# Reading the first expert's rows ahead of a branch, sending the last records behind all rows, and laying the pools in another order

## The chip, the cores and the metric

The kernel runs on one core of one Trainium2 chip. The metric is device time in microseconds (us) of the whole program; the time of a kernel is the median of its runs. The engines are named as the profile names them: PE (matrix multiply; PEld is its weight load), DVE (vector), ACT (scalar), POOL (GpSimd) and SP (sync, which here issues nearly all transfers).

## The reference, cut to what matters

```python
attn_out = attn(q, k, v, s)              # 4 x 8 heads, 576 tokens, head 64, causal, with a decay bias
x = attn_out as (4, 576, 512)            # 2304 tokens of 512
# mixture of experts: every token goes to one of 8 experts
fresh_e = argmax(logits[b, s]);  e = fresh_e or the token's predecessor's expert, by local_gate
h = max(x[b, s] @ w1[e], 0);  out[b, s] = p[e] * (h @ w2[e])         # 512 -> 1024 -> 512
# mixer
h = x.T @ U @ V;  u = x + h.T
result = u + max(u @ w_ch1, 0) @ w_ch2                               # 512 -> 2048 -> 512
```

All of it is float32. The kernel splits a float32 operand into a high part and a low part (`xh`, `xl`; `hh`, `hl`; the two halves of a `ring` tile) and multiplies three of the four pairs.

## The kernel before

The program has three stages on the time axis of the profile: attention with the router (0 to about 313 us), the experts (about 329 to 598 us) and the mixer (about 601 to 1020 us). No scheduler orders the instructions: within an engine they run as the code emits them, and in the attention stage the table `ORDER` gives that order job by job (`issue(ORDER)`).

**The router** sorts the tokens by expert. Experts are ranked by their count of tokens, and the rows of the fullest one, which is done first, go to a buffer in device memory, `x0_d` (the trace calls it `x_d`). For every tile of 128 tokens POOL sends two scattered transfers (L1220): the rows themselves (`send_x`) and a record per token with its number, factor and mixer entries (`send_sd`, into `sd_d`). The last two groups of tokens (of three and of two tiles) are sent from about 310 us on. Behind `issue(ORDER)` SP reads four raw tiles of the first expert's second weight (`raw_out`, L216).

**Between router and experts** a count of tokens per expert, `cnt`, is made on DVE (L1697). Every engine then reads words of it into registers (`values_load`, L1706 and L1714; TENSOR_LOAD in the trace) and reaches a branch, `tc.If(over >= 0)` at L1720. What it guards treats tokens beyond an expert's capacity; with these inputs no expert has any, and every engine jumps over the guarded code. Behind the guarded code each engine passes a few semaphore instructions of L1720 that close it. An accumulator of the guarded code, `a_ext`, is zero then; it is the first operand of `pu`, the mixer's partial sum, by a matmul at L1849.

**The experts' start** lies behind the branch. In the order of the code: four `conv` calls split the four raw tiles into `ring10` to `ring13` (ACT casts the high part, L230; DVE subtracts for the low part, L233); SP reads the first expert's rows, `xrow0` to `xrow2`, from `x0_d` (L1998); SP reads two more raw tiles (L216) and the records of the expert (`load_sd`, L1872); POOL splits those two tiles. Then, for each of the three row tiles, PE turns it (`trans_x`, four transposes into `xps`, L1896) and `split_x` makes `xh` on ACT (L1901) and `xl` on DVE (L1902). `ffn` then multiplies: for each of the 8 slices of the hidden dimension 12 matmuls into `ps_h` (L1618; two buffers), a Relu split into `hh` and `hl` (L1581, L1582), and matmuls into `acc` (L1630). The first `ps_h` matmul takes `xh`, the second takes `xl`, of all three row tiles.

**Where tiles lie.** Tiles live in pools that are laid one behind another in the on-chip memory. A pool that is closed gives its place to one opened later, and an instruction that writes a tile then waits for what still uses the old one. `xh`, `xl` and `xrow` stand in the pool `mp`, which is opened behind the closed pools `gp` (of the branch) and those of attention; `ring10` to `ring13` stand in `wfix`.

Of the kernel before, what the change touches and what calls it, by code (L numbers as in the profile page):

```python
# [12 lines left out]
F32 = mybir.dt.float32  # L13
# [114 lines left out]
def kernel(  # L128
# [179 lines left out]
    with ExitStack() as ax:  # L308
        ap = ax.enter_context(tc.tile_pool(name="at1", bufs=1))
        a2 = ax.enter_context(tc.tile_pool(name="at2", bufs=2))  # L310
        a3 = ax.enter_context(tc.tile_pool(name="at3", bufs=3))
        xpool = ax.enter_context(tc.tile_pool(name="xpool", bufs=6))
        rp = ax.enter_context(tc.tile_pool(name="rp", bufs=3))
# [8 lines left out]
        def job(eng, cost, fn, after=(), takes=(), frees=()):  # L322

            jobs.append((eng, cost, fn, [a for a in after if a is not None], takes, frees))
            return len(jobs) - 1

        def issue(order):

            assert sorted(order) == list(range(len(jobs)))
            freer = {}  # L330
            for i, j in enumerate(jobs):
                for f in j[5]:
                    freer.setdefault(f, i)
            out, taken = set(), {k: [] for k in PLACES}
            for i in order:
                _, _, fn, after, takes, _ = jobs[i]
                assert all(a in out for a in after)
                for k in takes:
                    old = len(taken[k]) - PLACES[k]
                    assert old < 0 or freer[taken[k][old]] in out  # L340
                    taken[k].append(i)
                fn()
                out.add(i)
# [1038 lines left out]
        prev, ready_, ends = {}, {}, []  # L1382
        for gi, (b, ts) in enumerate(groups):
# [29 lines left out]
            for eng, cost, i, f, fn in sends:  # L1413
                if f is send_x:
                    need, frees = [done["where"], init_, normed[ts[i]][1]], (normed[ts[i]][0],)
                else:
                    need, frees = [done["where"], done["factor"], done["sides"]], ()
                ends.append(job(eng, cost, fn, need, (), frees))
            ready_[gi] = [x for x in done.values() if not isinstance(x, list)] + ends[-len(sends):]
            prev = done  # L1420
        issue(ORDER)
# [6 lines left out]

    c1f = [wfix.tile([P, 512], I32, name=f"c1f{i}") for i in range(NF2)]
    c1u = [wfix.tile([P, 2, 512], F16, name=f"c1u{i}") for i in range(NF2)]  # L1430
# [237 lines left out]

    ux = ExitStack()
    psu = ux.enter_context(tc.tile_pool(name="psu", bufs=1, space=PSUM))  # L1670
    pu = psu.tile([P, DM], F32, name="pu")
    with ExitStack() as gx:
        gp = gx.enter_context(tc.tile_pool(name="gp", bufs=2))
        gs = gx.enter_context(tc.tile_pool(name="gs", bufs=2, space=PSUM))
        a_ext = gp.tile([P, DM], F32, name="a_ext", bufs=1)
# [28 lines left out]
        )  # L1704
        who = [0] + [
# [143 lines left out]
        nc.tensor.matmul(pu, lhsT=ident, rhs=a_ext, start=True, stop=False)  # L1849

    NH = NF + 2
    fj = ctx.enter_context(tc.tile_pool(name="fj", bufs=1, reuse_waits="tile"))
    al = wfix.tile([P, DM], F32R, name="al")
    with ExitStack() as mx:
        mp = mx.enter_context(tc.tile_pool(name="mp", bufs=1, reuse_waits="tile"))
# [4 lines left out]
        xh = mp.tile([P, KD, CAP], F32R, name="xh")  # L1860
        xl = mp.tile([P, KD, CAP], F32R, name="xl")
        xrow = [mp.tile([P, DM], F32, name=f"xrow{i}") for i in range(NC_T)]
# [132 lines left out]
        for f in range(NEARLY, NEARLY + 4):  # L1995
            conv(w2u[f], raw0.pop(f), False, nc.scalar, nc.vector)
        for i, xe in enumerate(xrow):
            nc.sync.dma_start(xe, x0_d[i * P : (i + 1) * P])  # L1998
# [6 lines left out]
        for i, m in tiles_of(0):  # L2005
            split_x(trans_x(xrow[i], ps1 if i == 2 else psx), i, m)
        nc.gpsimd.tensor_copy(idx, side[:, :, TID])
# [333 lines left out]
```

## Time and profile before

| | us |
|---|---|
| runs | 1025.58, 1022.31, 1022.51 |
| median | 1022.51 |
| profiled execution | 1021.61 |
| its span (first to last instruction) | 1019.9 |
| PE busy in it | 954.7 (94%) |
| DVE, ACT, POOL busy | 569.1, 454.2, 360.6 |

The profiled execution lies 0.90 us under the median, and 1.71 us of it lie outside its span. The profile gives each instruction a start and a duration, names for an engine's idle time the instruction that ended it, and gives for a stretch of time the clock that PE was granted, as a share of full speed. All starts are us from the start of the span.

### The profile page before, as it was taken

The numbers are of one execution on the slowest core, as the hardware profiler recorded it, in microseconds if no ns is written. First come the engines' busy times: TensorE is split into PE (matmuls) and PEld (weight loads), VectorE is DVE, ScalarE is ACT, GpSimd is POOL, SyncE is SP. The second block draws the span as 40 slices with busy tenths as digits, with TensorE's granted clock in tenths as the row PEclk, the third lists the DMA queues.
The fourth block names the chain that finished last, engine by engine and source line by source line (L and its number), as shares of the span: only waits on it lengthen the run. The fifth ranks groups of instructions, "written<-read, shape, count | busy, mean of one in ns | idle before, by whom it ended". The sixth has DMA issues, their size and how long they took to land.

```text
span 1019.9 us, 17854 instructions
## 1 busy us (share of the span) xinstructions
PE 954.7 (94%) x6566; PEld 761.4 (75%) x6566; DVE 569.1 (56%) x1124; ACT 454.2 (45%) x1031; POOL 360.6 (35%) x460
## 2 busy tenths in 40 slices
PE   5887999999994999999999969999999999999998
PEld 4786978888882989888888857887666666666676
DVE  6666786676784677677675966883112312311121
ACT  4766876667761456556555753332112112211111
POOL 6623636246475465665667622220000000000000
PEclk9878998779985899999999989999999999999999
DMA  7988999686523765666665421421000200100010
GB/s 171 195 182 177 217 213 224 141 187 149 128 64 121 217 202 188 212 196 204 187 180 169 147 100 62 146 63 51 33 1 1 83 1 1 61 2 0 1 42 21
DMA packets 127424, 120.79 MB, mean 118 GB/s; under 512 B 58407, under 2 KB 99687, under 8 KB 125536
## 3 DMA queue, kind: packets, MB, share of 16 engines
q1 hardware_dynamic: 119264, 105.64, 39.4%
q0 software_dynamic: 6864, 13.63, 4.8%
q8 instruction: 54, 0.88, 0.4%
q10 hardware_dynamic: 1200, 0.30, 0.1%
q14 instruction: 42, 0.34, 0.1%
HBM read 76.84 MB, written 22.30 MB: 97 GB/s over the span
## 4 chain that ended last, share of the span: by engine, by line
PE 64%; DMA 1%; ACT 1%; POOL 1%; DVE 1%; issue 1%; SPq 0%; DVEq 0%; ACTq 0%; POOLq 0%
PE acc L1630 31%; PE ps_h L1618 29%; PE pu L1987 2%; PE ups L2210 1%; PE xps L1896 1%; DMA raw_out<-in_moe_w_dram 1%; PE ph L2161 0%; ACT y L2058 0%; POOL ring L233 0%; DMA ut<-yt_d 0%; DMA yt_d<-y,idx 0%; POOL ug L1924 0%; DVE ul L2213 0%; SPq L1998 0%; DVE ut L2281 0%
## 5 line engine op out<-in xcount | busy, mean ns | idle before, releaser
L1630 PE MATMUL acc<-ring,hh 128*128 128x512 f32 x928 | 301.5, 406 | 0.0
L1582 DVE SCALAR_TENSOR_TENSOR hl<-ps_h,hh 128x512 fp32r<-128x512 f32 (+6 forms) x144 | 82.3, 572 | 253.2 <-ACT hh L1581 253.0
L1581 ACT ACTIVATE hh<-ps_h 128x512 fp32r<-128x512 f32 (+6 forms) x144 | 72.7, 505 | 338.3 <-PE ps_h L1618 338.1
L1630 PEld LDWEIGHTS acc<-ring,hh 128*128 128x128 f32 x928 | 167.1, 185 | 37.8
L1618 PE MATMUL ps_h<-uh,c1u 128*128 128x256 f16 (+1 forms) x768 | 192.8, 330 | 1.4 <-ACT uh L2212 1.4
L1630 PE MATMUL acc<-ring,hl 128*128 128x512 f32 (+4 forms) x464 | 183.2, 395 | 0.0
L1618 PEld LDWEIGHTS <-c1u 128*128 128x128 f16 x1152 | 108.3, 99 | 86.1 <-issue 21.9
L1618 PE MATMUL ps_h<-ul,c1u 128*128 128x256 f16 (+1 forms) x384 | 126.2, 329 | 0.9 <-DVE ul L2213 0.9
L1618 PE MATMUL ps_h<-xh,ring 128*128 128x384 f32 (+5 forms) x512 | 125.5, 318 | 0.7 <-ACT xh L1901 0.7
L233 POOL TENSOR_TENSOR ring<-raw_out,ring 128x512 fp32r<-128x512 f32 x60 | 81.1, 1352 | 76.3 <-ACT ring L230 74.9
L1630 PEld LDWEIGHTS acc<-ring,hl 128*128 128x128 f32 (+4 forms) x464 | 85.7, 185 | 22.3 <-DVE hl L1582 0.4
L788 DVE SCALAR_TENSOR_TENSOR lo<-pp,hi 128x384 f16<-128x384 f32 (+2 forms) x160 | 85.7, 550 | 21.7 <-ACT hi L783 20.1
L2202 POOL TENSOR_SCALAR us<-ut,up 128x512 f32<-128x512 f32 x9 | 6.7, 739 | 252.9 <-DVE up L2186 252.9
L1618 PEld LDWEIGHTS ps_h<-xh,ring 128*128 128x128 f32 x512 | 90.3, 192 | 3.7 <-ACT xh L1901 1.1
L783 ACT ACTIVATE hi<-pp 128x384 f16<-128x384 f32 (+2 forms) x160 | 77.2, 496 | 31.1 <-PE pp L775 28.4
L775 PE MATMUL pp<-ident,Pb 128*128 128x128 f32 x480 | 87.4, 307 | 1.9 <-DVE lo L788 0.7
L705 PE MATMUL sp<-OP 128*128 128x288 f32 (+4 forms) x192 | 75.3, 396 | 8.9 <-DMA OP<-parts 4.4
L746 ACT ACTIVATE Pb<-sp,nm 128x192 f32<-128x192 f32 (+4 forms) x160 | 80.9, 537 | 5.0 <-DVE nm L729 3.9
L1618 PE MATMUL ps_h<-xl,ring 128*128 128x384 f32 (+5 forms) x256 | 80.9, 316 | 0.6 <-DVE xl L1902 0.6
L729 DVE TENSOR_REDUCE nm<-sp 128x1 f32<-128x576 f32 (+4 forms) x96 | 67.7, 705 | 18.9 <-PE sp L720 18.3
L233 DVE TENSOR_TENSOR ring<-raw_in,ring 128x512 fp32r<-128x512 f32 x56 | 57.7, 1031 | 34.6 <-ACT ring L230 34.4
L230 ACT CAST ring<-raw_out 128x512 fp32r<-128x512 f32 x60 | 36.9, 619 | 68.0 <-PE acc L1630 40.4
(249 smaller groups left out, 1639.6 us busy)
## 6 DMA issues: line engine op xcount, KB each, us to landing
raw_in<-in_moe_w_dram SPq DMA_DIRECT2D x64, 256.0 KB, 3.7
raw_out<-in_moe_w_dram SPq DMA_DIRECT2D x64, 256.0 KB, 4.0
raw<-in_moe_w_ch_dram SPq DMA_DIRECT2D x32, 512.0 KB, 4.2
OP<-parts SPq DMA_DIRECT2D x28, 576.0 KB, 6.7
OP<-parts SPq DMA_DIRECT2D x28, 288.0 KB, 6.5
kn<-in_k_dram SPq DMA_DIRECT2D x32, 128.0 KB, 6.1
x_d<-x SPq DMA_DIRECT2D x16, 256.0 KB, 3.1
out_dram<-ut SPq DMA_DIRECT2D x4, 1024.0 KB
```

What stands on the lines that cost most here:

```text
L230: hi_eng.copy(hi, src)
L233: lo_eng.tensor_tensor(out=lo, in0=src, in1=hi.bitcast(F32), op=ALU.subtract)
L705: nc.tensor.matmul(sp[:, c, :cw], lhsT=W1[j][:, h, t * P : (t + 1) * P], rhs=K1[j][:, h, c0 : c0 + cw], start=True, stop=False,)
L729: nc.vector.tensor_reduce(out=k["nm"] if two else k["nm"][:, 0:1], in_=k["sp"], op=ALU.min, axis=AX.X if two else AX.XY,)
L746: nc.scalar.activation(out_, in_, AF.Exp, scale=-1.0, bias=k["nm"][:, x : x + 1])
L775: nc.tensor.transpose(pp[:, i - i0], k["pb"][:, a, x * P : (x + 1) * P], ident)
L783: nc.scalar.activation(k["hi"][:, i0:i1], k["pp", i0][:, : i1 - i0], AF.Copy, scale=SCALE)
L788: nc.vector.scalar_tensor_tensor(out=k["lo"][:, i0:i1], in0=k["pp", i0][:, : i1 - i0], scalar=SCALE, in1=k["hi"][:, i0:i1], op0=ALU.mult, ...
L1581: nc.scalar.activation(hh[:, :n], ps[:, :n], AF.Relu)
L1582: nc.vector.scalar_tensor_tensor(out=hl[:, :n], in0=ps[:, :n], scalar=0.0, in1=hh[:, :n].bitcast(F32), op0=ALU.max, op1=ALU.subtract,)
L1618: nc.tensor.matmul(ps[f][:, x * cut : (x + 1) * cut], lhsT=wa[:, kk], rhs=xa[:, kk, :cut], start=(kk == 0 and i == 0), stop=(kk == KD - 1 ...
L1630: nc.tensor.matmul(acc[i][0:m], lhsT=ha[:, sl], rhs=u2[g][:, wa], start=(g == 0 and jj == 0), stop=(g == nf - 1 and jj == 2),)
```

## The change

1. In attention the pools `xpool` and `rp` are laid first instead of last, and in `wfix` the tiles `c1u` come ahead of `c1f`. No instruction moves by it; the addresses do.
2. The record sends of the last two groups are taken out of `ORDER` and issued behind all other jobs.
3. The three reads of `xrow` stand ahead of the reads of `cnt` and the branch (after.py L1681), and so do the four `conv` calls. The pool `mp` with `xh`, `xl` and `xrow` is opened ahead of `gp`.
4. `a_ext` moves from `gp` to the tile `al` of `wfix`, and its matmul into `pu` stands behind the twelve transposes of the rows.

```diff
@@ attention's pools
+        xpool = ax.enter_context(tc.tile_pool(name="xpool", bufs=6))
+        rp = ax.enter_context(tc.tile_pool(name="rp", bufs=3))
         ap = ax.enter_context(tc.tile_pool(name="at1", bufs=1))
         a2 = ax.enter_context(tc.tile_pool(name="at2", bufs=2))
         a3 = ax.enter_context(tc.tile_pool(name="at3", bufs=3))
-        xpool = ax.enter_context(tc.tile_pool(name="xpool", bufs=6))
-        rp = ax.enter_context(tc.tile_pool(name="rp", bufs=3))
@@ the router's jobs
-        prev, ready_, ends = {}, {}, []
+        prev, ready_, ends, last_ = {}, {}, [], []
...
                 ends.append(job(eng, cost, fn, need, (), frees))
+                if late and f is not send_x:
+                    last_.append(ends[-1])
...
-        issue(ORDER)
+        issue([i for i in ORDER if i not in last_] + last_)
         raw0 = {f: load_out(0, f) for f in range(NEARLY, NEARLY + 4)}
@@ wfix
+    c1u = [wfix.tile([P, 2, 512], F16, name=f"c1u{i}") for i in range(NF2)]
     c1f = [wfix.tile([P, 512], I32, name=f"c1f{i}") for i in range(NF2)]
-    c1u = [wfix.tile([P, 2, 512], F16, name=f"c1u{i}") for i in range(NF2)]
@@ ahead of the branch
+    al = wfix.tile([P, DM], F32R, name="al")
+    mx = ExitStack()
+    mp = mx.enter_context(tc.tile_pool(name="mp", bufs=1, reuse_waits="tile"))
+    xh = mp.tile([P, KD, CAP], F32R, name="xh")
+    xl = mp.tile([P, KD, CAP], F32R, name="xl")
+    xrow = [mp.tile([P, DM], F32, name=f"xrow{i}") for i in range(NC_T)]
+    for i, xe in enumerate(xrow):
+        nc.sync.dma_start(xe, x0_d[i * P : (i + 1) * P])
...
+    a_ext = al.bitcast(F32)
     with ExitStack() as gx:
...
-        a_ext = gp.tile([P, DM], F32, name="a_ext", bufs=1)
         nc.vector.memset(a_ext, 0.0)
...
+        for f in range(NEARLY, NEARLY + 4):
+            conv(w2u[f], raw0.pop(f), False, nc.scalar, nc.vector)
         who = [0] + [
@@ behind the branch
-        nc.tensor.matmul(pu, lhsT=ident, rhs=a_ext, start=True, stop=False)
...
-        for f in range(NEARLY, NEARLY + 4):
-            conv(w2u[f], raw0.pop(f), False, nc.scalar, nc.vector)
-        for i, xe in enumerate(xrow):
-            nc.sync.dma_start(xe, x0_d[i * P : (i + 1) * P])
...
         for i, m in tiles_of(0):
             split_x(trans_x(xrow[i], ps1 if i == 2 else psx), i, m)
+        nc.tensor.matmul(pu, lhsT=ident, rhs=a_ext, start=True, stop=False)
```

What stands on the engines in a row, at three places. Numbers behind a name tell tiles of one name apart; `x0_d_70` is the rows' buffer in device memory, `sd_d_71` the records'.

POOL, the last sends of the router, before:

```order
L1220 DMA x0_d_70<-x_5277,pos_5503 2304x512
L1220 DMA x0_d_70<-x_5386,pos_5503 2304x512
L1220 DMA sd_d_71<-sd_5496,pos_5503 18432x40 x2
L1220 DMA x0_d_70<-x_5283,pos_5475 2304x512
L1220 DMA sd_d_71<-sd_5450,pos_5475 18432x40 x3
```

and after:

```order
L1221 DMA x0_d_70<-x_5277,pos_5503 2304x512
L1221 DMA x0_d_70<-x_5386,pos_5503 2304x512
L1221 DMA x0_d_70<-x_5283,pos_5475 2304x512
L1221 DMA sd_d_71<-sd_5450,pos_5475 18432x40 x3
```

The last send of rows stands ahead of all five sends of records instead of behind two of them; the two of `sd_5496` now come last.

SP, from the raw tiles to the branch, before:

```order
L216 DMA raw_out_5544<-in_moe_w2_dram 128x512
L1706 TENSOR_LOAD cnt_5622 x7
L1714 TENSOR_LOAD cnt_5622
L1720 COMPARE_AND_BRANCH
```

SP behind the guarded code, before:

```order
L1720 UNCONDITIONAL_BRANCH
L1998 DMA xrow0_7022<-x0_d_70 128x512
L1998 DMA xrow1_7023<-x0_d_70 128x512
L1998 DMA xrow2_7024<-x0_d_70 128x512
L216 DMA raw_out_7036<-in_moe_w2_dram 128x512
```

and SP after, from the raw tiles to the branch:

```order
L216 DMA raw_out_5544<-in_moe_w2_dram 128x512
L1681 DMA xrow0_5611<-x0_d_70 128x512
L1681 DMA xrow1_5612<-x0_d_70 128x512
L1681 DMA xrow2_5613<-x0_d_70 128x512
L1722 TENSOR_LOAD cnt_5636 x7
L1730 TENSOR_LOAD cnt_5636
L1736 COMPARE_AND_BRANCH
```

The three reads of rows have changed sides with the eight reads of `cnt` and the branch.

PE, from the guarded code to the first expert, before:

```order
L1849 MATMUL pu_5605<-a_ext_5612,ident_73 128x512
L1896 MATMUL xps_7047<-ident_73,xrow0_7022 128x128 x4
L1896 MATMUL xps_7054<-ident_73,xrow1_7023 128x128 x4
L1896 MATMUL xps_7061<-ident_73,xrow2_7024 128x128 x4
L1618 MATMUL ps_h_7080<-xh_7020,ring0_80 128x384
L1618 MATMUL ps_h_7080<-xl_7021,ring0_80 128x384
```

and after:

```order
L1903 MATMUL xps_7045<-ident_73,xrow0_5611 128x128 x4
L1903 MATMUL xps_7052<-ident_73,xrow1_5612 128x128 x4
L1903 MATMUL xps_7059<-ident_73,xrow2_5613 128x128 x4
L2010 MATMUL pu_5620<-al_5605,ident_73 128x512
L1621 MATMUL ps_h_7079<-xh_5609,ring0_80 128x384
L1621 MATMUL ps_h_7079<-xl_5610,ring0_80 128x384
```

The matmul into `pu` has passed the twelve transposes and stands directly ahead of the first `ps_h` matmul.

## Rows read from the trace of the kernel before

**Rows 1.** Page, part 1: PE's busy time, share of the span, instructions.

```profile
PE 954.7 (94%) x6566; PEld 761.4 (75%) x6566; DVE 569.1 (56%) x1124; ACT 454.2 (45%) x1031; POOL 360.6 (35%) x460
```

**Rows 2.** Timeline of PE at the experts' start: start, us, work [idle before <-what ended it].

```profile
322.03 2.04 PE L1849 MATMUL pu<-a_ext,ident 128*128 128x512 f32 x2 [8.52 <-DMA x_d<-x,pos]
325.00 1.09 PE L1896 MATMUL xps<-ident,xrow 128*128 128x128 f32 x4 [0.92 <-DMA xrow<-x_d]
326.66 1.97 PE L1896 MATMUL xps<-ident,xrow 128*128 128x128 f32 x8 [0.57 <-DMA xrow<-x_d]
329.31 0.69 PE L1618 MATMUL ps_h<-xh,ring 128*128 128x384 f32 x1 [0.67 <-ACT xh L1901]
330.60 0.69 PE L1618 MATMUL ps_h<-xl,ring 128*128 128x384 f32 x1 [0.61 <-DVE xl L1902]
```

**Rows 3.** Waits of PE from 331 to 600 us: total, times, longest.

```profile
PE pu L1987 <- ACT yh L2071: 2.7, 3, 1.4
```

**Rows 4.** Chain of waits that ends at 330.60: start, us, what.

```profile
324.43 3.99 DMA raw_out<-in_moe_w_dram
...
328.66 0.67 DVE xl L1902
```

**Rows 5.** Timeline of SP around the branch: start, us, transfers issued.

```profile
322.10 1.76 SPq L1998 DMA_DIRECT2D xrow<-x_d  x3
323.91 0.91 SPq L216 DMA_DIRECT2D raw_out<-in_moe_w_dram  x2
```

**Rows 6.** Timeline of POOL, the last sends: start, us, send, idle before.

```profile
316.40 0.97 POOL L1220 DMA_INDIRECT sd_d<-sd,pos  x1 [0.30 <-issue]
...
318.96 0.97 POOL L1220 DMA_INDIRECT x_d<-x,pos  x1 [0.30 <-issue]
320.24 0.97 POOL L1220 DMA_INDIRECT sd_d<-sd,pos  x1 [0.31 <-issue]
...
322.82 1.50 POOL L1220 DMA_INDIRECT sd_d<-sd,pos  x1 [0.30 <-issue]
```

**Rows 7.** Tile x_d, 309 to 323 us: from a send to its landing.

```profile
DMA to landing us min/median/max: 2.3/2.3/2.9
```

**Rows 8.** SP's reads of cnt: count, ns min/median/max, first and last start.

```profile
L1706 SPq TENSOR_LOAD <-cnt x7: 263/272/473, 315.7 to 317.8; - x7
```

**Rows 9.** The branch (L1720) by engine: count, ns min/median/max, first and last start.

```profile
L1720 SPq EVENT_SEMAPHORE  x9: 17/17/17, 321.1 to 321.7; - x9
L1720 POOLq EVENT_SEMAPHORE  x5: 17/43/5047, 322.3 to 327.6; - x5
L1720 ACTq EVENT_SEMAPHORE  x2: 17/17/17, 319.6 to 319.7; - x2
L1720 DVEq EVENT_SEMAPHORE  x2: 21/21/21, 320.7 to 320.8; - x2
L1720 PEldq EVENT_SEMAPHORE  x2: 51/51/51, 321.2 to 321.3; - x2
...
L1720 DVEq COMPARE_BRANCH  x1: 72/72/72, 317.6 to 317.6; - x1
L1720 SPq COMPARE_BRANCH  x1: 50/50/50, 318.5 to 318.5; - x1
```

**Rows 10.** Timelines of DVE and ACT around the branch: start, us, work.

```profile
320.98 2.50 DVE L233 TENSOR_TENSOR ring<-raw_out,ring 128x512 fp32r<-128x512 f32 x4 [5.36 <-DMA x_d<-x,pos]
328.66 1.89 DVE L1902 TENSOR_TENSOR xl<-xps,xh 128x512 fp32r<-128x512 f32 x3 [5.18 <-DMA raw_out<-in_moe_w_dram]
...
319.91 2.18 ACT L230 CAST ring<-raw_out 128x512 fp32r<-128x512 f32 x4 [10.32 <-DMA sd_d<-sd,pos]
```

**Rows 11.** Stretches of PE: us, busy (instructions), granted clock, DMA share, GB/s.

```profile
610.90:616.50 5.60, 5.59 (x27) 0.50 0.00 1
...
330.60:336.60 6.00, 6.00 (x19) 0.50 0.97 290
336.70:339.70 3.00, 3.00 (x19) 1.00 0.84 245
```

More of the change, by code (lines that the diff above doesn't have):

```diff
@@ L1665, in ffn @@
         return acc
+    NH = NF + 2
+    fj = ctx.enter_context(tc.tile_pool(name="fj", bufs=1, reuse_waits="tile"))
+    al = wfix.tile([P, DM], F32R, name="al")
[6 more added lines that the diff above has]
+        nc.sync.dma_start(xe, x0_d[i * P : (i + 1) * P])
     ux = ExitStack()
@@ L1847 @@
                     )
-        nc.tensor.matmul(pu, lhsT=ident, rhs=a_ext, start=True, stop=False)
[L1851 to L1855, printed above, removed]
+    with mx:
         m3 = mx.enter_context(tc.tile_pool(name="m3", bufs=3, reuse_waits="tile"))
@@ L1859 @@
         psx = mx.enter_context(tc.tile_pool(name="psx", bufs=2, space=PSUM, reuse_waits="tile"))
-        xh = mp.tile([P, KD, CAP], F32R, name="xh")
-        xl = mp.tile([P, KD, CAP], F32R, name="xl")
-        xrow = [mp.tile([P, DM], F32, name=f"xrow{i}") for i in range(NC_T)]
         def tiles_of(j):
```

## The prediction

> **What bounds the kernel now.** I read the busy times first. PE works for 954.7 us, 94% of the span [rows 1], so a gain must be found where PE waits, or where its clock is low. Then the waits of PE from the experts' start on: behind 331 us the longest entry in its list is 2.7 us in three waits [rows 3], and so what starts there earlier also ends earlier: a gain at the start of the experts carries to the end at full size. Third, PE's timeline of that start [rows 2]. The reader is to see five pieces with a gap ahead of each: 8.52 us of waiting for the router's sends and the branch, `pu` at 322.03, a gap of 0.92 until the first row tile is there (325.00), 0.57 until the others are (326.66), 0.67 until `xh` is made, and 0.61 until `xl` is. From 330.60 on PE runs without gaps. Without that last gap the same row would have begun at 330.60 - 0.69 = 329.91; this is the moment that I compare with.
>
> What holds each piece? The chain of waits [rows 4] names for the last gap a transfer of `raw_out`, issued at 324.43 and landed 3.99 later; `xl` doesn't read it. The tile `xl` lies on a place that the branch's pool had, and waits for transfers of the time before. The rows themselves hang on `xrow`, issued from 322.10 on [rows 5]. Two things end there nearly at once: SP comes out of the branch (semaphore instructions until 321.7 [rows 9]), and the last send of rows, started at 318.96 [rows 6], lands 2.3 to 2.9 us later [rows 7], at 321.3 to 321.9. Neither alone would bring much; the change moves both.
>
> **The sends.** On POOL the last send of rows takes the place of a record send at 316.40 instead of 318.96 [rows 6]: 2.56 us earlier, with landing at 318.7 to 319.3. The number of sends is the same, so the last ends where it did, and POOL's part of the branch's end, which waits for the landings until 327.6 [rows 9], stays.
>
> **The reads of the rows.** SP now meets them ahead of its reads of `cnt`. It has nothing else to do then: those reads begin at 315.7 [rows 8], when `cnt` is there. So `xrow` goes out when the last send has landed. If the landing was what held it before (2.9), it goes 2.56 earlier, at 319.5; if the branch held it (2.3), it goes at 318.9, 3.2 earlier. I take 2.8 between the two, 319.3. Queued behind it on SP are seven reads of `cnt` of 0.27 us each and the branch. Before, this was 315.7 to 318.5, then the jump until 321.1 and semaphores until 321.7 [rows 8, 9]: 2.8 + 2.6 + 0.6 = 6.0. The three reads take 1.76 [rows 5], so SP comes out at 319.3 + 1.8 + 6.0 = 327.1, and the two `raw_out` behind it go out 3.2 later than 323.91. Who waits for that is POOL, which splits them into tiles needed six and seven slices later, each many microseconds long, and the first Relu, below.
>
> **The transposes.** From the issue to the first tile it took 325.00 - 322.10 = 2.9 us, to the others 326.66 - 322.10 = 4.6. Moved rigidly by 2.8, PE turns the first tile at 322.2 and the others from 323.9 to 325.8. If all landed 2.9 after their own issue, the end would be 325.2. PE is out of the branch at 321.3 and ACT at 319.7 [rows 9], before that. DVE needs a look: its four `conv` subtracts, 2.50 us [rows 10], now stand ahead of its branch, which it reached at 317.6 and left at 320.8; it will leave at about 323.3, which is ahead of the third tile's transposes and of `xl`. ACT's four casts [rows 10] fall into an idle stretch of 10.32 us and cost nothing.
>
> **The matmul into `pu`.** It moves 2.04 us [rows 2] from a stretch in which PE waited to one in which it could work, so by itself it costs. It covers the making of `xh` (0.67) and `xl` (0.61), whose false wait is gone since `mp` no longer lies on the branch's pool. The first `ps_h` matmul comes at 325.8 + 2.04 = 327.9, with the better landings at 327.3, and nothing waits behind it. Against 329.91 that is 2.0 to 2.6 earlier; I take 2.3. The sum in parts: 2.8 for the rows, 0.67 and 0.61 for the two gaps, less 2.04, makes 2.0, and 0.3 for a part of the better landings.
>
> **The clock.** PE was granted half speed until 336.60, 6.00 us behind the start of the row without gaps, and there 19 matmuls took 6.00; behind it 19 took 3.00 [rows 11]. The same was seen at the other low place: dense from 610.9, full from 616.5, 5.60 later. So each microsecond at the low level costs half of one. Before, 336.60 - 329.91 = 6.7 us of the experts' work were done low. Now the row without gaps is longer ahead of the first `ps_h`. If `pu` counts in it, it starts at 325.8 and the clock returns at about 331.8, 3.9 behind 327.9: 2.8 fewer low, worth 1.4. If only the experts' matmuls count, 6.0 are low and 0.35 is won; if the transposes from 323.9 count too, 2.0 are low and 2.35 is won. I take 1.4, the middle.
>
> **Addresses.** The reordered pools and `c1u` ahead of `c1f` add no instruction; they serve that `conv` and `xrow` can run early without a wait for a late tile of attention. Their price is nothing by itself; if they fail, that is the second rival below.
>
> **The sum.** 2.3 + 1.4 = 3.7 us. The profiled execution has 1021.61, so 1017.9; the median of the runs lies 0.90 above that execution, which makes 1018.8. The ends of the unknowns: 2.0 + 0.35 = 2.35 and 3.0 (reads at 318.9 with the better landings) + 2.35 = 5.35, that is 1020.2 and 1017.2.
>
> **The rivals.** First, *a new last wait eats a part*. The send at 316.40 now lies beside the four subtracts of DVE, which would run from about 315.7 to 318.2. Before, these subtracts (320.98 to 323.48) lay beside three record sends of 0.97, 1.00 and 1.50 [rows 6, 10]: at most 0.53 was lost, and the sends kept their spacing of 1.3. So I price this at 0 to 0.53. Were a send held until the subtracts are done, it would start at 318.2, 1.8 later, and leave 3.7 - 1.8 = 1.9: 1020.6. [...] To the same case belong a landing of a row tile slower than before by 1 to 2 us and a DVE that leaves its branch later than the third tile is turned. They leave 1 to 2.6, at 1019.9 to 1021.5. For it speaks that 4.6 us for the later tiles already show transfers in each other's way.
>
> Second, *the rows don't come earlier*: something else (a place in memory that a late tile still holds) keeps `xrow` until about 322. Then the transposes end at 328.63 as before, `pu` runs until 330.7, 0.8 behind 329.91, and the clock, counted from `pu` as above, gives back 1.4: a gain of 0.6, at 1021.9. Against it: the waits of the moved reads in the built program are those for the sends alone.
>
> Third, on the other side, *SP comes out of the branch too late*. The first Relu waits for SP's part of the branch's end; SP now waits for the rows' landing ahead of its jump. PE can fill two `ps_h` tiles, 24 matmuls of 0.316 [rows 11], from 327.9 to 335.5, before it needs the first Relu's result, which takes some 0.6. The loss begins when SP comes out later than 334.9, against my 327.1; it cancels the gain from 338.6 on, 11.5 later than I reckon, and each microsecond behind that makes the kernel one slower than before. It needs a jump or a landing several times longer than any in the rows (jumps of 2.6 to 3.1 for SP and DVE, landings up to 3.99), so it is unlikely.
>
> **How the numbers follow.** The forecast has 0.62, the new last wait 0.21, rows not earlier 0.10, SP too late 0.07. What a measurement of this kernel can tell from no change is about 0.3%, 3.07 us: faster means below 1019.4. The forecast lies 0.6 below that; of its 0.62 I put 0.54 below and 0.08 above, where the clock gives little. Within 0.3% falls that 0.08, with the first two rivals and 0.01 of the last: 0.40. Slower gets 0.06. The range takes in the ends of the sum and the first rival; it leaves out the last rival and most of the second, some 0.16, and reaches from 1017.0 to 1021.6.
>
> **What the profile of the changed kernel would show.** The last send of rows at 316.4, not 318; `xrow` issued at 319 to 319.5 (322 would be the second rival); transposes from about 322.2; `pu` directly behind them, and the first `ps_h` at 327.3 to 327.9 with no gap behind; the granted clock full from about 331 to 332 (333.9 would take away 1.0 of the gain); SP out of its branch near 327, and no wait of PE for a Relu before 336. Wrong would be a gap of PE behind the first `ps_h` matmul, or a time outside the range.

## The result, and the profile after

The changed kernel takes 1014.23 us (median of 6 runs, 1007.95 to 1017.78), the kernel before beside it 1024.42 (6 runs). The ratio of the two is 0.9903, with a 95% interval of 0.9881 to 0.9926: some 9.9 us faster. That is the forecast direction, but 2.7 times the 3.7 us forecast, and it lies below the range. The runs of the changed kernel also spread over 10 us, those of the kernel before over 3.

The profiled execution of the changed kernel took 1015.48 us, with a span of 1013.5: 6.4 less than the span before. PE's line of the page beside [rows 1]:

```profile
PE 936.4 (92%) x6566; PEld 743.1 (73%) x6566; DVE 567.8 (56%) x1124; ACT 453.6 (45%) x1031; POOL 361.6 (36%) x460
```

To see where the 6.4 us lie, cut both spans at two instructions of DVE: the one that ends `cnt`, behind all of attention and the router, and the one that reads `pu` for the mixer, behind all experts. DVE's timelines, before first (start, us, work):

```profile
315.46 0.16 DVE L1697 TENSOR_SCALAR cnt<-cnt 1x8 int32<-1x8 int32 x1
...
600.64 0.68 DVE L2103 TENSOR_TENSOR mix<-pu,mix 32x512 fp32r<-32x512 f32 x1 [0.51 <-ACT mix L2102]
```

and after:

```profile
309.87 0.16 DVE L1711 TENSOR_SCALAR cnt<-cnt 1x8 int32<-1x8 int32 x1
...
595.22 0.68 DVE L2107 TENSOR_TENSOR mix<-pu,mix 32x512 fp32r<-32x512 f32 x1 [0.51 <-ACT mix L2106]
```

| us | before | after | difference |
|---|---|---|---|
| start to `cnt` ready (attention, router) | 315.62 | 310.03 | -5.6 |
| `cnt` ready to `pu` read (the handover and the experts) | 285.02 | 285.19 | +0.2 |
| `pu` read to the end (mixer) | 419.26 | 418.29 | -1.0 |

So in this pair of profiles nearly all of the gain lies in attention, where no instruction moved but for the last sends, and none in the stretch from `cnt` to `pu`, at which the moved instructions aim ("the stretch" below; a number with a plus, such as +9.3, is us behind `cnt`). In the first 300 us PE was granted a mean of 0.93 of full speed instead of 0.88, and was busy 256.40 us instead of 266.09 (stretches: us, PE busy, clock, DMA share, GB/s; before, then after):

```profile
0.00:300.00 300.00, 266.09 (x2934) 0.88 0.79 172
```

```profile
0.00:300.00 300.00, 256.40 (x2979) 0.93 0.74 173
```

The handover itself did change. PE's timeline after, beside [rows 2]:

```profile
319.33 2.79 PE L1903 MATMUL xps<-ident,xrow 128*128 128x128 f32 x12 [11.38 <-DMA xrow<-x_d]
321.91 1.27 PE L2010 MATMUL pu<-al,ident 128*128 128x512 f32 x2
322.80 0.57 PE L1621 MATMUL ps_h<-xh,ring 128*128 128x384 f32 x1
323.52 0.44 PE L1621 MATMUL ps_h<-xl,ring 128*128 128x384 f32 x1 [0.16 <-DVE xl L1909]
...
333.85 0.44 PE L1621 MATMUL ps_h<-xh,ring 128*128 128x384 f32 x1 [1.77 <-DVE hl L1585]
```

Transposes, `pu` and `ps_h` now follow each other with one gap of 0.16 instead of three of 0.57 to 0.67. But the transposes begin 319.33 - 310.03 = 9.30 us behind `cnt`; before it was 325.00 - 315.62 = 9.38. And 11 us on there is a new gap of 1.77. The clock came back much earlier, at about 322.4, 12.4 behind `cnt` instead of 21.0 (stretches of PE after, beside [rows 11]):

```profile
300.00:322.30 22.30, 7.40 (x39) 0.50 0.31 98
322.50:336.00 13.50, 11.57 (x59) 1.00 0.64 183
```

### The profile page after: what moved, and what is told of

Read it like the earlier page. It is cut to its first block, busy times and chain, and to the rows that moved or that the text cites. A ratio compares the mean times of both kernels' runs of the same rounds, so it can differ in the third digit from the quotient of the medians.

```text
span 1013.5 us, 17840 instructions
## 1 busy us (share of the span) xinstructions
PE 936.4 (92%) x6566; PEld 743.1 (73%) x6566; DVE 567.8 (56%) x1124; ACT 453.6 (45%) x1031; POOL 361.6 (36%) x460
## 4 chain that ended last, share of the span: by engine, by line
PE 63%; DMA 2%; DVE 1%; ACT 1%; issue 1%; SPq 0%; POOL 0%; DVEq 0%; ACTq 0%; POOLq 0%
PE acc L1633 31%; PE ps_h L1621 28%; PE pu L1994 2%; PE ups L2214 1%; DMA raw_in<-in_moe_w_dram 1%; PE xps L1903 1%; DMA raw_out<-in_moe_w_dram 0%; PE ph L2165 0%; DVE c1u L1536 0%; DMA yt_d<-y,idx 0%; DMA ut<-yt_d 0%; ACT y L2062 0%; DVE ul L2217 0%; POOL ring L233 0%; DVE ut L2285 0%
## 5 line engine op out<-in xcount | busy, mean ns | idle before, releaser
L776 PE MATMUL pp<-ident,Pb 128*128 128x128 f32 x480 | 83.8, 297 | 4.7 <-DVE lo L789 2.6
L706 PE MATMUL sp<-OP 128*128 128x288 f32 (+4 forms) x192 | 71.8, 379 | 7.9 <-DMA OP<-parts 3.2
L713 PE MATMUL sp<-OP 68*128 68x288 f32 (+4 forms) x192 | 61.4, 324 | 2.2 <-DMA OP<-b_d 2.2
## 6 DMA issues: line engine op xcount, KB each, us to landing
OP<-parts SPq DMA_DIRECT2D x28, 288.0 KB
```

The source lines that it names most:

```text
L706: nc.tensor.matmul(sp[:, c, :cw], lhsT=W1[j][:, h, t * P : (t + 1) * P], rhs=K1[j][:, h, c0 : c0 + cw], start=True, stop=False,)
L713: nc.tensor.matmul(sp[:, c, :cw], lhsT=W2[j][0:SK, h, t * P : (t + 1) * P], rhs=K2[j][0:SK, h, c0 : c0 + cw], start=False, stop=not diag,)
L776: nc.tensor.transpose(pp[:, i - i0], k["pb"][:, a, x * P : (x + 1) * P], ident)
```

## The experiments

Three questions: what made attention shorter; why the rows came no earlier; and what the moved instructions are worth in the end. Ratios are to the kernel before in the same series of runs, since the kernel before itself took 1014 to 1022 us in the other series; the absolute times expected of the first four kernels were reckoned from the 1024 of the result, but the kernel before took 1016.33 beside them, so only the ratios are compared.

**What made attention shorter.** The reordered pools move attention's pool `at1` (its tiles `kn`, `qn`, `vn` and `OP` are filled by transfers) from byte 69024 of each partition to 96000: from 160 past a multiple of 256 to a multiple of 256. Two kernels move only that pool, one moves it back in the changed kernel, and one makes the first part of the change alone. The shift, ahead of `at1` (a second one behind it makes the two add up to 512 bytes for all that follows):

```diff
+        pada = ax.enter_context(tc.tile_pool(name="pada", bufs=1))
+        pada.tile([P, 24], F32, name="pada")
         ap = ax.enter_context(tc.tile_pool(name="at1", bufs=1))
```

The kernel before, shifted by 96:

> The kernel before, with 96 unused bytes per partition laid ahead of the pool at1 and 416 behind it; no instruction moves. at1 holds attention's tiles that transfers fill (kn, qn, vn, OP); it began at byte 69024, 160 past a multiple of 256, and begins at 69120, a multiple of 256, as in the changed kernel (96000). Theory A: the addresses make attention shorter (in the first 100 us the packets of the hardware queue took 53.6 ns each before, 75.2% of 16 engines for 22456 packets, and 47.3 ns after, 68.0% for 22980; cnt was ready 5.6 us earlier). It expects packets near 47 ns, cnt ready at 306 to 312 us instead of 315.5, and a time of 1014 to 1020. Rival B: attention's shorter time is chance of one profile or comes from the order of the code, and the gain is that of the moved reads: 53 ns, cnt at 315, 1022 to 1026.

The kernel before, shifted by 32 (`[P, 8]`):

> The kernel before, with 32 unused bytes ahead of at1 and 480 behind: at1 begins at 69056, a multiple of 64 but 192 past a multiple of 256. If a multiple of 64 is what the transfers want, it does as the shift by 96 does (packets near 47 ns in the first 100 us, 1014 to 1020). If it is a multiple of 256, packets stay at 52 to 55 ns and the time at 1021 to 1026. Rival B expects 1022 to 1026 too, but then for the shift by 96 as well.

The changed kernel, shifted by 160 (`[P, 40]`):

> The changed kernel, with 160 unused bytes ahead of at1 and 352 behind: at1 begins 160 past a multiple of 256 again, as in the kernel before; all instructions stand as changed. Theory A: attention is as long as before (cnt ready at 314 to 317 us, packets near 53 ns), and what is left is the gain of the moved reads, sends and pu, 0 to 4 us by what the trace of the changed kernel shows (7.0 earlier at the first ps_h matmul of which 5.6 are attention's, 3.3 of clock, and some 4 lost again to waits until 373 us): 1019 to 1024. Rival B: 1012 to 1017 as the changed kernel.

The pools alone, that is the kernel before with the first point of the change and nothing else:

> The kernel before with the first part of the change alone: xpool and rp laid first, c1u ahead of c1f. at1 begins at 96000, a multiple of 256. Theory A: as the shift by 96, 1014 to 1020, cnt ready at 306 to 312. Rival B (the gain comes from the reads ahead of the branch): 1022 to 1026, cnt at 315.

Measured: 0.9937 (0.9901 to 0.9972) for the shift by 96; 0.9996 (0.9969 to 1.0023) for the shift by 32; 0.992 (0.9888 to 0.9953) for the pools alone; 0.9994 (0.9965 to 1.0022) for the changed kernel shifted off. `cnt` was ready at 304.95, 312.24, 309.05 and 311.18 in their profiles; the last lies below the 314 to 317 that were expected of it. Over all profiles of this document it was 304.8 to 314.5 with `at1` at a multiple of 256 (13 profiles, mean 309.6) and 311.2 to 315.6 off it (four, mean 313.1), so a single pair of profiles, like that of the result, shows little. The transfers separate the kernels clearly. The row of the hardware queue over the first 100 us (packets, MB, share of 16 engines), for before, after, the shifts by 96 and by 32, and the changed kernel shifted by 160:

```profile
q1 hardware_dynamic: 22456, 15.20, 75.2%
```

```profile
q1 hardware_dynamic: 22980, 15.51, 68.0%
```

```profile
q1 hardware_dynamic: 22980, 15.51, 68.4%
```

```profile
q1 hardware_dynamic: 22243, 14.86, 75.8%
```

```profile
q1 hardware_dynamic: 22966, 15.50, 75.5%
```

Share times 16 engines times 100 us, by packets: 53.6, 47.3, 47.6, 54.5 and 52.6 ns a packet. All kernels with `at1` at a multiple of 256 lie at 47 to 49, all others at 52.6 to 54.5. The rival, that the moved reads made the whole gain, falls: without the addresses 0.6 us is left of it, give or take 3, and the addresses alone give most. A multiple of 64 wasn't enough (54.5 ns a packet, 0.9996). A start 128 past a multiple of 256 was not tried, so these runs can't tell a boundary of 256 bytes from one of 128.

The higher clock of the first pair, 0.93 against 0.88 over the first 300 us, can't be put down to the addresses: over all profiles it was 0.89 to 0.94 with `at1` at a multiple of 256 and 0.88 to 0.93 off it (0.89 in `e3_pools_only`, 0.93 in `q_moves` below). In which waits of attention the shorter packets save time wasn't followed.

**Do more addresses help?** The raw weights, too, begin 160 past a multiple of 256. `f1_all_aligned` is the changed kernel with all bulk tiles at multiples of 256:

```diff
+    padc = ctx.enter_context(tc.tile_pool(name="padc", bufs=1))
+    padc.tile([P, 24], F32, name="padc")
     wring = ctx.enter_context(tc.tile_pool(name="wring", bufs=1))
...
+        pada = ax.enter_context(tc.tile_pool(name="pada", bufs=1))
+        pada.tile([P, 40], F32, name="pada")
         ap = ax.enter_context(tc.tile_pool(name="at1", bufs=1))
...
     al = wfix.tile([P, DM], F32R, name="al")
+    wfix.tile([P, 24], F32, name="padw")
```

> The changed kernel with unused bytes laid in (96 ahead of wring, 160 ahead of at1, 96 at the end of wfix), so that all tiles that transfers fill or empty in bulk begin at multiples of 256: the raw weights (160 past one before and changed), the x rows (160 past one in the changed kernel), xrow and the raw tiles of the mixer's weights (64 past one). If the addresses matter for these too, attention is 0 to 2 shorter than in the changed kernel, the landings of raw tiles are shorter, the waits of PE among the experts (0.5 to 4 us in the changed kernel) shrink, and the time is 2 to 5 below the changed kernel's (0.980 to 0.988 of the kernel before). If only attention's small packets mind, it is as the changed kernel (0.988 to 0.993).

Measured 0.9908 (0.9877 to 0.9938), as the changed kernel. The raw weights' packets are of 512 and 2048 bytes, and they took as long as elsewhere: from 340 to 580 us a mean of 27.5 and 96.6 ns, against 27.6 and 95.2 in the changed kernel and 27.7 and 97.3 before. `f0_before_all_aligned` has the same addresses, with all instructions in the old order:

> The kernel before with the pools of the change and the unused bytes of f1_all_aligned, but no instruction moved: all addresses are good, sends, reads, conv and pu stand as before. If the addresses are the whole gain: 0.989 to 0.992 as f1. If the moved instructions give 1.5 to 3 us besides (the stretch from cnt to the end of the experts was 285.1 in the mean of four kernels with the old order, 283.6 in three with the new, and the mixer 0.9 shorter): 0.992 to 0.995, and the stretch is 284.8 to 285.5.

Measured 0.9921 (0.9892 to 0.9951); its stretch was 288.0, out of what was expected. I come back to that.

**Why the rows came no earlier.** The last send of rows did start 2.5 us earlier, 0.81 behind `cnt` instead of 3.34. After, POOL's row, and SP's rows at the reads (count, ns min/median/max, first and last start):

```profile
310.84 1.25 POOL L1221 DMA_INDIRECT x_d<-x,pos  x1 [0.30 <-issue]
```

```profile
L1681 SPq EVENT_SEMAPHORE  x4: 28/28/702, 315.7 to 316.2; - x4
L1681 SPq DMA_DIRECT2D xrow<-x_d x3: 4/688/712, 316.9 to 317.7; - x3
```

SP is let go at 315.7, 4.9 us behind the send's start, where landings before took 2.3 to 2.9; then one semaphore instruction of SP took 0.70. The reads went out 6.9 behind `cnt`, where it had been 6.5. In the eight profiles with the reads ahead of the branch, the old send order among them, they went out at 5.3 to 6.9. Undoing the send order in the changed kernel:

```diff
-        issue([i for i in ORDER if i not in last_] + last_)
+        issue(ORDER)
```

> The changed kernel with the sends in the old order, so that the last send of rows starts 3.3 us behind cnt instead of 0.8. Theory C: the earlier send gains nothing because its landing takes 4.9 instead of 2.9 us; here it lands about +6.3, the reads go out at +6.5, the transposes stand at +9.2 to +9.8 as in the changed kernel, and the stretch from cnt to the end of the experts is 282 to 286 (SP later by 0 to 1). Rival D: the transposes come 2.5 later than in the changed kernel, at +11.5 to +12, and the stretch grows by 2 to 2.5.

Measured: reads at +6.2, transposes at +9.5, stretch 284.4, ratio 0.9923 (0.9897 to 0.9949). SP was let go 2.5 behind the last send's start here, and the rows came as early: theory C holds, the earlier send by itself gains nothing. What holds its landing up can be read off the traces. Between 312.7 and 314.5, when the last rows' packets were due, the transfers of the changed kernel were (queue, kind: packets, MB, share of 16 engines over 1.8 us):

```profile
q0 software_dynamic: 95, 0.03, 7.2%
q8 instruction: 1, 0.02, 6.1%
```

One packet of 16 KB of instructions held one engine for 6.1% of 16 x 1.8 us = 1.75 us, in the time in which PE jumped. It ended at +4.467; of the send's seven packets of 4096 bytes all but two were under way by +2.9, the next began at +4.473, and the last ended at +5.2. Before, the last packet of this send, which started 2.5 later, ended at +5.3. All nine profiles with the changed order of sends have it so: the last but one of the packets begins 5 to 8 ns behind the end of the packet of instructions (+3.95 to +4.47). None of the eight with the old order has it, since there these packets move from +4.9 on, when that packet is gone. That the two stand in the queue of one engine is inferred from these times; the profile doesn't name the engine. That PE's jump calls for the packet is inferred from times too: PE's branch took 4.13 us here and 3.73 before, and in both profiles one packet of that queue lies within it, before between 318.6 and 319.7 us (PE's branch after and before: count, ns min/median/max, first and last start).

```profile
L1736 PEldq COMPARE_BRANCH  x1: 4130/4130/4130, 311.8 to 311.8; - x1
```

```profile
L1720 PEldq COMPARE_BRANCH  x1: 3732/3732/3732, 317.4 to 317.4; - x1
```

Reading no sent rows at all shows what rows in time would be worth. `k1_rows_no_wait` leaves out the dependence, and with it the right rows of the first expert:

```diff
-        nc.sync.dma_start(xe, x0_d[i * P : (i + 1) * P])
+        nc.sync.dma_start(xe, x_d[i * P : (i + 1) * P])
```

> The changed kernel with the three rows read from x_d, the buffer of all tokens in their own order, which is written long before, instead of x0_d; so the reads wait for no send, and the first expert works on other rows than it should. It shows what rows that are there in time are worth. The transposes then wait for PE alone, which left its branch 5.3 to 6.0 us behind cnt: they stand at +5.5 to +6.5 instead of +9.3, SP leaves its branch at +5.5 to +7, and the first ps_h stands at +9 to +10.5. The stretch from cnt to the end of the experts is then 279 to 282. If something besides the rows holds the transposes (ACT or DVE out of the branch), they stay at +8 to +9.3.

Measured: `cnt` ready at 314.47, transposes at 320.56, so +6.1, right behind PE's branch:

```profile
320.56 2.79 PE L1903 MATMUL xps<-ident,xrow 128*128 128x128 f32 x12 [8.16 <-DMA sd_d<-sd,pos]
323.15 1.92 PE L2010 MATMUL pu<-al,ident 128*128 128x512 f32 x2
324.95 0.69 PE L1621 MATMUL ps_h<-xh,ring 128*128 128x384 f32 x1
```

The stretch was 278.9, some 5 us shorter than the mean of the changed order's others, as expected; only SP came out of its branch at +9.8 instead of +5.5 to +7. So in this one profile earlier rows do carry through the experts; in the changed kernel they just weren't earlier. The time, 0.9883 (0.9827 to 0.9938) from two runs, isn't clear of the changed kernel's. `h1_reads_behind` puts the reads back behind the branch:

```diff
-    for i, xe in enumerate(xrow):
-        nc.sync.dma_start(xe, x0_d[i * P : (i + 1) * P])
...
+        for i, xe in enumerate(xrow):
+            nc.sync.dma_start(xe, x0_d[i * P : (i + 1) * P])
         for f in range(NEARLY + 4, NF):
```

> The changed kernel with the three reads of rows back behind the branch; all else as changed. Counted from the moment cnt is ready on DVE, the first transposes stood at +9.4 before, +9.3 in the changed kernel and +9.2 in the changed kernel with the shift by 160, with SP out of the branch at +6 before and +15.8 changed. Theory C: the last landing of rows comes at about +5.7 in the changed kernels, since its packets wait behind code that the jumping engines fetch, so reads behind the branch go out as early (+6.2); the transposes stay at +9 to +9.7, the raw reads of SP go out at +8 instead of +15.8, and the wait of PE for hl near 332 us (1.8 us) is gone: the stretch from cnt to the end of the experts (mix read from pu; 285.0 before, 285.2 changed, 281.9 changed and shifted) is 280.5 to 282.5. Rival D, the prediction's: the reads ahead of the branch bring the rows forward; without them the transposes stand at +11 to +12 and the stretch is 284 to 287.

Measured 0.9932 (0.9903 to 0.9961). Its profile, of the longest of its ten executions, had the reads at +9.7, the transposes at +12.4 and a stretch of 288.5. Theory C fails here, and so does its rival's reason, for `f0` in the old order showed the same: reads at +9.9. There SP came out of its jump in time, and then took 3.9 us from the first to the last of its nine semaphore instructions, in steps of up to 0.7 (317.1 to 321.0, with `cnt` ready at 311.30):

```profile
L1724 SPq EVENT_SEMAPHORE  x9: 4/17/709, 317.1 to 321.0; - x9
```

Is that the kernel's or the run's? The same program once more:

> The same program as f0_before_all_aligned. In its first profile SP's semaphore instructions behind the branch took 0.7 us each, so that the rows' reads went out 9.9 us behind cnt and the stretch from cnt to the end of the experts was 288.0, while three kernels with the same order of instructions (before, the shift by 96, the pools alone) had reads at +6.5 and 284.9 to 285.1. If these slow instructions come and go from run to run, the second profile has reads at +6.5 and 284.8 to 285.5; if they belong to the addresses of this kernel, +9.7 to +10 and 287.5 to 288.5. The ratio to the kernel before stays in 0.989 to 0.995 either way; a value of 0.992 to 0.995 again leaves 1 to 3 us to the moved instructions (changed kernel 0.990, all aligned 0.991).

```profile
L1724 SPq EVENT_SEMAPHORE  x9: 17/17/17, 310.6 to 311.2; - x9
```

Now reads at +6.7 and a stretch of 283.6: it comes and goes from run to run. The ratio was 0.997 (0.9935 to 1.0005), out of the 0.989 to 0.995 expected, in a series in which the kernel before took 1014.38. With the reads behind the branch, the slow instructions hold the rows up by 3 us (three of eight profiles); with the reads ahead, as in the changed kernel, they lie around the reads, with one of 0.702 ahead of them and two of the reads themselves slow (the 0.688 and 0.712 in the rows above).

**The new gap of 1.77 us.** `hl` is late. What holds it, on DVE and ACT after:

```profile
331.86 1.46 DVE L233 TENSOR_TENSOR ring<-raw_in,ring 128x512 fp32r<-128x512 f32 x1 [4.92 <-ACT ring L230]
333.25 0.55 DVE L1585 SCALAR_TENSOR_TENSOR hl<-ps_h,hh 128x384 fp32r<-128x384 f32 x1
```

```profile
331.21 0.62 ACT L230 CAST ring<-raw_in 128x512 fp32r<-128x512 f32 x1 [4.86 <-DMA raw_in<-in_moe_w_dram]
331.73 0.49 ACT L1584 ACTIVATE hh<-ps_h 128x384 fp32r<-128x384 f32 x1
```

On ACT the second Relu, `hh` (331.73), runs behind the cast of a raw weight of the next expert (331.21), which waited 4.86 us for its transfer. SP issued that read at 327.72, since it left the branch only at 325.7: its eight reads of `cnt` stood behind the wait for the rows. `k2_reads_behind_counts` is `f1` with the three reads between the reads of `cnt` and the branch:

```diff
-    for i, xe in enumerate(xrow):
-        nc.sync.dma_start(xe, x0_d[i * P : (i + 1) * P])
...
+        for i, xe in enumerate(xrow):
+            nc.sync.dma_start(xe, x0_d[i * P : (i + 1) * P])
         with tc.If(over >= 0):
```

> The changed kernel with all bulk tiles at multiples of 256 (as f1_all_aligned) and the three reads of rows moved behind SP's eight reads of cnt, still ahead of its branch. In the changed kernels SP left its branch 13.7 to 15.2 us behind cnt, since the reads of cnt stood behind the wait for the rows, and the raw weights of the second expert went out late, which cost PE waits for hl of 0.2 to 2.0 us. Theory: the eight reads of cnt (2.8 us) now fit into that wait; the rows go out as before (+5.3 to +6.9), SP leaves at +10 to +12.5, the waits for hl vanish, the stretch from cnt to the end of the experts is 281 to 283 instead of 283.8 (f1), and the time is 0 to 3 us below f1's: 0.986 to 0.991 of the kernel before. Rival: the stretch's differences (281.9 to 285.2 in the three changed kernels) are not SP's; then 283 to 285 and 0.990 to 0.993.

Measured: no wait of PE for `hl`, a stretch of 282.8 and 0.9904 (0.9867 to 0.994). The mechanism is as thought; the time isn't clear of `f1`'s.

**What brings the clock back.** `pu` ahead of the transposes again, in the changed kernel:

```diff
+    nc.tensor.matmul(pu, lhsT=ident, rhs=a_ext, start=True, stop=False)
     with mx:
...
-        nc.tensor.matmul(pu, lhsT=ident, rhs=a_ext, start=True, stop=False)
```

> The changed kernel with the matmul into pu back ahead of the transposes. The clock was granted in full from +12.4 and +12.8 behind cnt in the two changed kernels that were profiled, and from +17.7 to +21 in the four with the old order. Theory: transposes, pu and ps_h in a row without gaps are what brought it back 5 to 8 us sooner (worth 2.5 to 4 us). Without pu in the row the first ps_h comes 1 to 1.5 earlier (+11.3 to +11.8), gaps of 0.3 to 0.7 return ahead of ps_h, and the clock returns later, at +15 to +21: the stretch from cnt to the end of the experts is 0 to 3 longer. Rival: the clock's return has to do with something else (the removed wait of xl); then it stays at +12 to +13 and the stretch is 1 shorter.

Measured: full clock at 323.3, 17.5 behind `cnt`; the gap ahead of `ps_h` is back; the first `ps_h` stands at +12.8, not earlier; the stretch, 283.7, is no longer than the others'; 0.9936 (0.9905 to 0.9966). So the row of `pu` does bring the clock back sooner, but what it brings is within the spread of the stretch.

```profile
312.00:323.20 11.20, 8.89 (x27) 0.50 0.40 120
323.40:336.00 12.60, 12.60 (x67) 1.00 0.82 241
```

All profiles agree on this: with `pu` between transposes and `ps_h` and the reads early, the clock was full 12.1 to 15.8 behind `cnt` (eight profiles), with `pu` ahead 17.5 to 22.6 (eight). In `h1_reads_behind`, with `pu` in the row but late rows and a gap of 1.14 among the transposes, it was 21.3.

**What belongs to which part.** Three kernels side by side, with the kernel before (1021.43) as the fourth corner:

> The kernel before with at1 shifted by 96 bytes to a multiple of 256, once more, beside the two others of this call. If the addresses carry the most: 0.990 to 0.996; the stretch from cnt to the end of the experts 284.8 to 285.5 as in the other kernels with the old order.

> The changed kernel with at1 shifted by 160 bytes off the multiple of 256: the moved instructions alone. If they give the 1.5 to 3 us that the stretch from cnt to the end of the experts and the mixer's shorter start show (281.9 to 285.2 against 283.6 to 285.5; 0.9): 0.996 to 0.9985. If they give nothing: 0.999 to 1.001. The forecast, 3.7 us, would be 0.9964.

> The changed kernel beside the two others. If the parts add up, its distance to the kernel before is the sum of theirs: 0.988 to 0.993. Its stretch from cnt to the end of the experts shows whether the 285.2 of its first profile, with waits of PE for hl and for raw_out, is its rule (284.5 to 286) or one of several (281.9 to 284).

| part | ratio (95%) | ns a packet | reads | transposes | full clock | `cnt` to `pu` read |
|---|---|---|---|---|---|---|
| addresses (`q_addresses`) | 0.9943 (0.9915 to 0.997) | 48.2 | +9.9 | +12.6 | +22.6 | 287.3 |
| moves (`q_moves`) | 0.9974 (0.9945 to 1.0003) | 53.8 | +6.8 | +9.5 | +14.2 | 285.0 |
| both (`q_both`) | 0.9886 (0.9851 to 0.992) | 48.3 | +6.8 | +9.3 | +15.1 | 284.2 |

In us that is 5.8, 2.7 and 11.6; the two parts make 8.5, within the interval of both. The addresses are half of the 11.6 and two thirds of the 8.5. The moves alone gave 2.7 here and 0.6 in the first series, with intervals of some 3 us either way that take in no change; on top of the addresses they make 11.6 - 5.8 = 5.8 here. A gain of them is likely, its size isn't settled. The stretch points the same way: 281.9 to 285.2, mean 284.0, in the five profiles with all moves as changed; 283.6 to 288.0, mean 285.6, in the seven with all in the old order.

## Why the prediction was right in direction and wrong in size

The direction was luck in large part: the addresses, priced at nothing, brought most of the gain, and what the moves alone brought isn't clear of no change.

- **Addresses: the step that failed.** The prediction said of the reordered pools that "their price is nothing by itself". No row stood behind that nothing. They were worth 3 to 8 us in five comparisons, half to two thirds of the whole. I had looked at which tile lies on which, and not at where each begins; the trace of before had a sign in it, packets of a mean 53.6 ns in attention, which I had no reason to compare with anything. The range had no room for a change in a stage in which no instruction moved.
- **The sends.** Start 2.5 earlier, as said. The landing, taken at 2.3 to 2.9, was 4.9 in this profile, behind the packet of instructions. The first rival's cause (transfers in each other's way) and the second rival's outcome (rows not earlier) together: the transposes stood at +9.2 to +9.5 in all five profiles of the changed order, instead of the forecast 322.2 - 315.62 = +6.6. This term, 2.8, was nothing.
- **The send beside DVE's subtracts.** The send beside the four `conv` took 1.25 to 1.27 instead of 0.97, in every kernel with `conv` ahead of the branch: some 0.3, in the bound of 0 to 0.53. No run shows the first rival's full hold of 1.8.
- **The gaps and `pu`.** As forecast: the false wait of `xl` is gone, `pu` covers the making of `xh` and `xl`, with 0.16 left over. The `ps_h` matmul with `xl` stands at +13.5 instead of +15.0. Of the 2.3 for the start about 1.5 came in this profile, and all from this row, since the twelve transposes also run as one piece.
- **The clock.** Right that a row without gaps brings it back sooner, sized too small. I took full speed 3.9 behind the first `ps_h`; it came 0.4 ahead of it in the first profile and 0 to 2.4 behind it in the seven others with `pu` in the row and early rows (3.9 in `h1_reads_behind`), against 7.3 before. Of my three cases the one that counts the transposes comes nearest: the clock was full 3.1 to 6.3 behind the first of them in the eight profiles, 3.1 in the first. The 6.00 that I carried over from before isn't fixed; why it differs stays open. In the first profile all 6.7 low microseconds were won, worth 3.3 by that reckoning instead of 1.4.
- **SP out of the branch.** Forecast 327.1 on a clock in which `cnt` is ready at 315.6, that is +11.5; it was +15.7, since the rows came later and SP's instructions were slow. The third rival had the place and the mechanism of queueing, but not the way: the first Relu did wait 3.11 us for SP, until 325.86, but PE still had work; what held PE up was the raw weight of the next expert in ACT's and DVE's queues. It cost 1.77 in this profile and 0.6 to 1.5 in the four others of that order.
- **Waits behind.** "And nothing waits behind it" was wrong. A second wait of PE, of 0.85 us, ends at 366.29; the chain of waits ahead of it (start, us, what) shows a raw weight of 3.86 us ahead of ACT's casts, `y` and `yh`, for which PE waits (last, PE's own row):

```profile
358.94 3.86 DMA raw_out<-in_moe_w_dram
362.90 0.52 ACT ring L230
363.42 1.84 ACT y L2062 x3
...
365.52 0.64 ACT yh L2075
```

```profile
366.29 0.71 PE L1994 MATMUL pu<-yh,ug 128*128 128x512 f32 x2 [0.85 <-ACT yh L2075]
```

  The experts' start, earlier than its weights, only waited for them later: in the first profile the first matmul into `acc` stood 4.15 us earlier behind `cnt` than before (329.81 against 339.55 on the two axes), and the first into `pu` by an expert only 0.27 (366.29 against 372.15). Of the 3.88 lost between them 2.94 are idle time of PE, which had none there before; in the rest it was busy longer, 33.54 instead of 32.60. So the stretch came out 0.2 longer than before. In the four others of this order it was 0 to 3.1 shorter.
- **The mixer** was 0.8 to 1.2 shorter in four of the five profiles with the changed order; it was so once in the old order too (418.3), so I don't count it as the change's.

## What to carry to other kernels

When pools or tiles move, compare the addresses at which tiles filled by transfers begin, modulo 256, before any order of instructions: packets of 256 bytes paid most for it here (22.7 to 24.3 ns instead of 18.2 to 19.4), and it cost a few unused bytes to mend. The reads issued ahead of the branch were only as early as the slowest thing in their way (+6.9 instead of +6.5, behind a landing of 4.9 us), and what was queued behind them on SP got later (out of the branch at +15.7 instead of +6.1); put what doesn't depend on them (here the reads of `cnt`) first. And where a run's clock and transfers spread by 10 us, price a step by the distance between two of its own instructions, and judge the whole by kernels run side by side.

## What the runs showed of the hardware that I had not expected

- **Transfers into `at1`'s tiles were slower when these didn't begin at a multiple of 256 bytes.** 52.6 to 54.5 ns a packet against 47 to 49 over the first 100 us, the same instructions, addresses apart by 32 to 160 bytes; a start 192 past a multiple of 256, itself a multiple of 64, wasn't enough. By size, means of the hardware queue's packets in the 13 profiles on a multiple and the four off it: 256 bytes 18.2 to 19.4 ns against 22.7 to 24.3, 2304 bytes 150 to 156 against 169 to 172, 9216 bytes 682 to 694 against 713 to 724. In five comparisons this was worth 0.3% to 0.8% of this kernel's time. What makes them slower isn't shown: of the 256-byte packets 53% to 64% took at most 19 ns off the boundary too (89% to 98% on it), and the raw weights' packets of 512 and 2048 bytes took the same either way (27.5 to 27.7 and 95.2 to 97.3 ns).
- **SP's instructions, plain semaphore ones too, went on in steps of up to 0.7 us in some runs**, for about 3.5 us from 6 us behind `cnt` (317.1 to 321.0 in `f0_before_all_aligned`), and in steps of under 0.1 in others of the same program (310.6 to 311.2 in `f0_second_look`). What causes it stays open; since the same program had both, it isn't the kernel alone.
